# Mixing the heads of an attention score on quarters of the TensorE array, with keys in chunks of 128, 128, 128 and 64

## Chip, cores and metric

One NeuronCore of a Trainium2 chip runs the whole program in one launch. The metric is the device time of that launch in microseconds (us), lower is better; a time is the median of several runs.

## What is computed

Talking-heads attention feeds a mixture of experts (`moe`) and a second one (`moe2`). The change lies wholly in the attention:

```python
batch, n_heads, seq, head_dim = (4, 12, 448, 64)
scores = scale * np.matmul(q, k.transpose(0, 1, 3, 2))
scores = np.einsum('bhij,hg->bgij', scores, w_pre)      # pre-mix over the 12 heads
scores = scores - np.max(scores, axis=-1, keepdims=True)
attn = np.exp(scores)
attn = attn / (np.sum(attn, axis=-1, keepdims=True) + 1e-09)
attn = np.einsum('bhij,hg->bgij', attn, w_post)         # post-mix over the 12 heads
return np.matmul(attn, v).astype(np.float32)
```

All in float32. The result, 1792 tokens of 768 features, goes to `_moe_ref` and `_moe2_ref`, which stay as they are.

## The kernel before

`phase_a` is the attention, and the later phases are the two mixtures. Tokens are taken in tiles of at most 120 (three of 120 and one of 90 for each of the 4 batches, 16 in all). For a tile:

- `q_prep` and `k_prep` turn q (and, once a batch, k) with TensorE transposes and split them in a high and a low part; `scores` (L367) multiplies them in three matmuls for each head, two heads at a time on the two row halves of the array.
- Each head's scores (tokens x 448 keys) are copied to SBUF (`ss`) and sorted by a DMA (L386) into `s2`, so that 120 partitions hold 10 tokens x 12 heads. 12 such units of 10 tokens make a tile (9 in the short one), 180 in all.
- `pre` (L417) mixes the heads of one unit: one 120 x 120 matmul with the block matrix `kron_pre` over 448 keys. `top` (L420, VectorE) takes the maximum of each row, `exp` (L424, ScalarE) the exponential and its sum.
- Three units (30 tokens) make a group. `fin` (L440 to L442, VectorE) divides the block matrix of the post-mix by the sums, which gives `wc`. `post` (L455) has the exponentials of a chunk of 112 keys as weights and `wc` as the moving operand, so that the result has keys on partitions; 4 chunks x 3 units = 12 matmuls of 120 columns for a group, 720 in all. Each chunk of a group is copied from PSUM to `am` (L228 on VectorE, L229 on ScalarE).
- When a tile is whole, `av_mul` (L481) multiplies with v: 12 heads x 4 chunks, two heads side by side on the two column halves of the array.

Beside this, `narrow` turns the float64 weights of the first mixture to float32 in 64 pieces (DMA in, four to six small instructions on ScalarE, VectorE and POOL, DMA out).

A float32 matmul is two records in the trace, each with its weight load; a matmul on a part of the array runs beside its neighbours on the other parts.

The order on every engine is made by `Plan.schedule`: each operation has a cost, a due time (counted in groups), the buffers that it takes and the operations that it depends on; the engine that is free first takes the ready operation that is due first. The costs and due times say only in which order the instructions are written; each engine then runs its own list in order and waits at semaphores. `mode` names how the array is split ("" whole, "rows", "cols"), and `STAY` puts off an operation that would change it. PSUM has 8 banks, dealt out as 2 for `pre`, 2 for `post` and 4 for the rest.

The program begins with `build_kron`, which loads the two small mixing matrices with DMAs issued by ScalarE and builds the block matrices on VectorE.

## Time and profile before

| | us |
|---|---|
| time before, median of 3 runs (893.16 to 899.93) | 894.21 |
| the profiled execution, its own time | 892.66 |
| its span in the trace | 890.9 |
| of it the attention, to the first matmul of the first mixture | 487.4 |
| TensorE (PE) busy in the attention | 471.26 |
| VectorE (DVE) busy in the attention | 366.48 |
| ScalarE (ACT) busy in the attention | 337.42 |

The page of the profile gives busy times by engine and by line for the whole span. The later phases begin at 487.4 us, so the tables by stretch of time tell the stages apart; the timeline shows instructions one after the other with the idle time ahead of each and what ended it; the table of waits sums that idle time by what was waited for. PEld is TensorE's weight load, which runs beside the matmul. The end of a matmul is modelled, so what one costs in a row of its like is read from start to start: a merged row of n records that lasts T, with a mean duration d of one record, has (T - d) / (n - 1) from one start to the next.

### The profile page before, as it was taken

What the parts mean: (1) busy time and instruction counts of PE and PEld (TensorE: products, weight loads), DVE (VectorE), ACT (ScalarE), POOL (GpSimd) and SP (SyncE); (2) the same over time, 40 slices, a digit from 0 to 9 for tenths busy, and PEclk for the clock granted to TensorE, in tenths of its full rate; (3) what the DMA queues carried; (4) which work ended last, traced back from release to release, by engine and by line L of the source; (5) the groups of instructions that cost most, each with busy time, mean ns of one, the idle gap of its engine ahead of it and who ended that gap; (6) DMA issues with size and microseconds to landing.
All of it is one profiled execution on the core that took longest, in us unless ns stands there. A gap on an engine that the chain in (4) does not pass through costs nothing.

```text
span 890.9 us, 17763 instructions
## 1 busy us (share of the span) xinstructions
PE 839.7 (94%) x6636; PEld 606.2 (68%) x6636; DVE 622.2 (70%) x1279; ACT 501.6 (56%) x1119; POOL 180.3 (20%) x275
## 2 busy tenths in 40 slices
PE   7798999999999999999999999999999998989764
PEld 5576777787677777777678767776776787834112
DVE  4658788788977689787844878876777888833003
ACT  5557768666867676776755444454445556502003
POOL 2323344334533344334400000000000000010000
PEclk9999999999999999999999999999999999999878
DMA  7999988998999997999576792553554458899998
GB/s 164 205 195 240 226 239 223 255 233 185 218 236 247 233 235 201 227 228 235 161 210 139 185 192 79 183 189 118 176 186 143 142 183 249 309 349 414 415 375 310
DMA packets 179666, 198.92 MB, mean 223 GB/s; under 512 B 71296, under 2 KB 153186, under 8 KB 179580
## 3 DMA queue, kind: packets, MB, share of 16 engines
q1 hardware_dynamic: 164824, 159.18, 62.0%
q0 software_dynamic: 14496, 38.60, 19.9%
q8 instruction: 52, 0.85, 0.4%
q14 instruction: 34, 0.28, 0.1%
q10 hardware_dynamic: 260, 0.01, 0.0%
HBM read 135.40 MB, written 23.59 MB: 178 GB/s over the span
## 4 chain that ended last, share of the span: by engine, by line
PE 72%; DMA 12%; DVE 6%; ACT 4%; SPq 3%; issue 2%; POOL 1%; ACTq 0%; DVEq 0%; POOLq 0%
PE po L455 13%; PE pre L417 12%; PE h L715 8%; PE av L481 8%; PE h L716 7%; PE h L718 7%; PE s L367 5%; DMA s<-ss 4%; PE eh L1095 2%; DMA wf<-w 2%; DMA raw<-in_moe_w_in_dram 2%; PE p L837 2%; DMA ring<-in_moe_w_dram 2%; DMA early<-in_moe_w_dram 1%; SPq L1002 1%
## 5 line engine op out<-in xcount | busy, mean ns | idle before, releaser
L455 PEld LDWEIGHTS po<-wc,e 120*112 120x112 f32 x1440 | 171.7, 177 | 65.7 <-issue 46.0
L455 PE MATMUL po<-wc,e 120*112 120x120 f32 x1440 | 183.4, 269 | 3.3 <-ACT am L229 2.5
L417 PE MATMUL pre<-s,kron_pre 120*120 120x448 f32 x360 | 167.8, 552 | 6.0 <-ACT e L424 4.2
L420 DVE TENSOR_REDUCE mz<-pre 120x1 f32<-120x448 f32 x180 | 111.4, 620 | 49.8 <-PE pre L417 48.5
L715 PE MATMUL h<-x,wh 128*128 128x512 f32 (+1 forms) x384 | 139.7, 373 | 3.4 <-ACT wh L667 3.4
L716 PE MATMUL h<-x,wh 128*128 128x512 f32 (+1 forms) x384 | 136.7, 365 | 0.0
L424 ACT ACTIVATE e<-pre,mz 120x448 f32<-120x448 f32 x180 | 114.6, 637 | 27.6 <-DVE mz L420 25.8
L386 POOL DMA_DIRECT2D s<-ss x180 | 106.3, 592 | 112.9 <-ACT ss L229 72.8
L229 ACT COPY am<-po 112x360 f32<-112x360 f32 x183 | 84.3, 462 | 50.7 <-PE po L455 49.1
L557 POOL TENSOR_TENSOR nar<-nar,cvt 128x384 uint32<-128x384 uint32 x64 | 64.0, 1000 | 146.1 <-DVE cvt L548 59.8
L715 PEld LDWEIGHTS h<-x,wh 128*128 128x128 f32 x384 | 72.2, 188 | 30.9 <-ACT cg L729 9.2
L718 PE MATMUL h<-x,wf 128*128 128x512 f32 (+1 forms) x384 | 87.8, 364 | 0.0
L729 ACT ACTIVATE cg<-h 128x512 int32<-128x512 f32 (+1 forms) x64 | 34.6, 541 | 92.3 <-PE h L718 92.3
L716 PEld LDWEIGHTS h<-x,wh 128*128 128x128 f32 x384 | 72.2, 188 | 11.2
L481 PE MATMUL av<-am,v 112*64 112x120 f32 (+1 forms) x1536 | 77.6, 261 | 0.0
L481 PEld LDWEIGHTS av<-am,v 112*64 112x64 f32 x1536 | 74.1, 137 | 2.1 <-issue 0.3
L718 PEld LDWEIGHTS h<-x,wf 128*128 128x128 f32 x384 | 66.7, 188 | 11.9
L730 DVE SCALAR_TENSOR_TENSOR cg<-h,cg 128x512 f32<-128x512 f32 (+1 forms) x64 | 39.6, 619 | 46.1 <-ACT cg L729 46.1
L417 PEld LDWEIGHTS pre<-s,kron_pre 120*120 120x120 f32 x360 | 52.5, 183 | 22.1 <-ACT e L424 13.7
L668 DVE TENSOR_TENSOR wf<-wf,wh 128x768 fp32r<-128x768 f32 x64 | 61.0, 953 | 9.2 <-ACT wh L667 9.1
L737 ACT ACTIVATE cg<-cg,consts 128x512 f32<-128x512 f32 (+1 forms) x64 | 42.9, 671 | 35.9 <-DVE cg L732 35.6
L229 ACT COPY ss<-s 120x448 f32<-120x448 f32 (+1 forms) x114 | 55.6, 537 | 10.7 <-DMA s<-ss 8.0
(173 smaller groups left out, 1138.4 us busy)
## 6 DMA issues: line engine op xcount, KB each, us to landing
s<-ss POOLq DMA_DIRECT2D x144, 210.0 KB, 8.4
early<-in_moe_w_dram SPq DMA_DIRECT2D x36, 768.0 KB
wf<-w SPq DMA_DIRECT2D x64, 384.0 KB
raw<-in_moe_w_in_dram SPq DMA_DIRECT2D x32, 384.0 KB
w<-nar SPq DMA_DIRECT2D x64, 192.0 KB
raw<-in_moe_w_out_dram SPq DMA_DIRECT2D x32, 384.0 KB
gn<-in_moe_w_dram SPq DMA_DIRECT2D x16, 768.0 KB
early<-w SPq DMA_DIRECT2D x16, 384.0 KB
```

What stands on the lines that cost most here:

```text
L229: return nc.scalar.copy(out=out, in_=in_)
L386: QUEUE[e].dma_start(out=s2t[ti][h::12, :n // 10], in_=x[h][:n])
L417: nc.tensor.matmul(prt[gi, c][:, :S], kpre, s2t[ti][:, 3 * g + c, :], start=True, stop=True)
L420: nc.vector.tensor_reduce(out=mz[gi][:, 0, c:c + 1], in_=prt[gi, c][:, :S], axis=AX.X, op=ALU.max, negate=True)
L424: nc.scalar.activation(out=et[gi][:, c, :], in_=prt.pop((gi, c))[:, :S], func=AF.Exp, bias=mz[gi][:, 0, c:c + 1], accum_out=mz[gi][:, 1, c ...
L455: nc.tensor.matmul(pt[:, :360].rearrange("p (g i) -> p g i", i=30)[:, :, 10 * c:10 * c + 10], et[gi][:, c, jt * CJ:(jt + 1) * CJ], wct[gi] ...
L481: nc.tensor.matmul(pt[64 * o:64 * o + 64, x * 120:x * 120 + n], vt[:, g, jt, :], am[ti % 2][:, g, jt, :n], start=(jt == 0), stop=(jt == NJ ...
L557: nc.gpsimd.tensor_tensor(out=f, in0=f, in1=x["t"], op=ALU.add)
L668: nc.vector.tensor_tensor(out=wf_t[v], in0=wf_t[v].bitcast(F32), in1=wh.bitcast(F32), op=ALU.subtract)
L715: nc.tensor.matmul(pt, wh[:, c], xh[:, c, :], start=(c == 0), stop=False)
L716: nc.tensor.matmul(pt, wh[:, c], xl[:, c, :], start=False, stop=False)
L718: nc.tensor.matmul(pt, wl[:, c], xh[:, c, :], start=False, stop=(c == 5))
```

## The change

Four things are changed together:

- **Pre-mix on quarters.** The sorted scores stand on partitions 4 to 123, and the 4 partitions before them are filled with zeros once. So the first 5 tokens of a unit end at partition 63 and the other 5 begin at 64. `pre` takes two units at once as four matmuls of 64 columns (60 of them in use), each on one quarter of the array: row half r holds 5 tokens of each unit, column half u is the unit. The results lie in two PSUM banks with 120 rows in use of 128. 88 such pairs and 4 single units (whole array) take the place of 180 matmuls.
- **Keys in chunks of 128, 128, 128 and 64.** `post` runs over three full chunks; the chunk of 64 (`post_half`) is made for two groups at once, six heads on each column half of the array. `av_mul` has three full chunks and, ahead of them, the half chunk on quarters of the array. k and v are loaded and turned in the same chunks.
- **Groups of 40 tokens** (of 20, 30 or 40 in the short tile): 48 groups in place of 60. `fin`, the copies and `wc` are as much wider.
- **PSUM banks by the plan.** All 8 banks are one pool; the planner gives each operation the bank that is free first, at most 6 for `pre`, 3 for `post` and 4 for the rest. Due times are set anew.

Matmuls, by the built programs: `pre` 180 before, 352 on quarters (88 sets of four) and 4 whole after; `post` 720 before, 540 with 128 keys and 360 with 64 keys (180 side by side pairs) after; `av` 768 before, 576 and 192 on quarters (48 sets of four) after; scores and transposes of q as before. Copies to `am`: 240 before (183 on ScalarE, 57 on VectorE), 180 after (137 and 43). In the list of TensorE the way in which the array is split changes 123 times before the first mixture begins, and 207 times after the change.

The core of the diff ("..." where lines are left out):

```diff
-PLACES = {"pre": 2, "post": 2, "ps": 4, "knat": 2, "qnat": 2, "ssrc": 8, "s2": 2, "e": 3, "wc": 2, "xst": 1,
-          "raw": 4, "nar": 5, "cv_t": 3}
-SPARE = 3 * ["ps", "pre", "ps", "post", "ps", "pre", "ps", "post"]
-
-K_DUE, S_DUE, S_SPAN, P_DUE, AV_DUE, AV_SPAN, STAY = 5.6, 4.8, 1.9, 1.9, 0.0, 1.0, 0.6
+PLACES = {"knat": 2, "qnat": 2, "ssrc": 8, "s2": 2, "e": 5, "mz": 4, "wc": 2, "xst": 1, "raw": 4, "nar": 5, "cv_t": 3}
+BANKS, MOST = 8, {"pre": 6, "post": 3, "ps": 4}
+
+K_DUE, S_DUE, S_SPAN, P_DUE, AV_DUE, AV_SPAN, STAY = 4.8, 4.8, 2.5, 2.45, 0.3, 0.5, 0.45
...
-N_FIRST, N_LAST = 5.5, 55.0
+PAIRED = 2
+N_FIRST, N_LAST = 5.5, 56.5
...
-    nc.scalar.dma_start(out=wb, in_=w.unsqueeze(0).to_broadcast([10, 12, 12]))
+def build_kron(nc, pool, ident, w, scale, name, inner):
...
+    wb = pool.tile([128, 12], F32, name=f"wb_{name}")
+    nc.vector.memset(wb, 0.0)
+    m = pool.tile([128, 2, 5], F32, name=f"m_{name}")
+    for u in range(2):
+        p = slice(64 * u, 64 * u + 60) if inner else slice(4 + 60 * u, 64 + 60 * u)
+        nc.scalar.dma_start(out=wb[p], in_=w.unsqueeze(0).to_broadcast([5, 12, 12]))
+        nc.vector.tensor_reduce(out=m[:, u], in_=ident[:, p].rearrange("p (i h) -> p i h", i=5), axis=AX.X, op=ALU.add)
     if scale != 1.0:
         nc.vector.tensor_scalar(out=wb, in0=wb, scalar1=scale, scalar2=None, op0=ALU.mult)
...
+    kr = pool.tile([128, 120 if inner else 128], F32, name=f"kron_{name}")
+    if inner:
+        out = [(kr.rearrange("p (g i) -> p g i", i=10), m.rearrange("p u i -> p (u i)"))]
+    else:
+        nc.vector.memset(kr, 0.0)
+        out = [(kr[:, 64 * u:64 * u + 60].rearrange("p (i g) -> p g i", i=5), m[:, u]) for u in range(2)]
...
 
     ROWS = [120, 120, 120, 90]
-    NG = [4, 4, 4, 3]
+    UNITS = [[[2, 2], [2, 2], [2, 2]]] * 3 + [[[2, 2], [2], [2, 1]]]
...
+        s2 = [sg.tile([128, 12, S], F32, name=f"s2_{i}") for i in range(2)]
+        nc.vector.memset(s2[0][:4], 0.0)
+        nc.gpsimd.memset(s2[1][:4], 0.0)
+        vh = sl.tile([2 * HJ, H // 2, D], F32, name="v_half")
...
+        amt = [sl.tile([CJ, 120 * H * NJ + 60 * H], F32, name=f"am{i}") for i in range(2)]
+        am = [t[:, :120 * H * NJ].rearrange("p (g t i) -> p g t i", g=H, t=NJ) for t in amt]
+        ah = [t[:, 120 * H * NJ:].rearrange("p (g i) -> p g i", g=H // 2) for t in amt]
...
-            return PSUMS[slot.tag_used].tile([128, 512], F32, tag=slot.tag_used, name=name)
+            return ps.tile([128, 512], F32, tag=f"bank{slot.bank}", name=name)
...
+                n, keys = (CJ, slice(t, CJ * NJ, NJ)) if t < NJ else (HJ, slice(CJ * NJ, S))
                 nc.sync.dma_start(
-                    out=knat[b, half][:, t],
-                    in_=k[b, 6 * half:6 * half + 6, t::NJ, :].rearrange("h p d -> p h d"))
-            kload[b, half, t] = dma(0.55, 0.9, start, due=due, late=3.0 if b else 0.0, takes=[] if t else [kslot[b, half]],
+                    out=knat[b, half][:n, t],
+                    in_=k[b, 6 * half:6 * half + 6, keys, :].rearrange("h p d -> p h d"))
...
+                if c < 3:
+                    ins = nc.sync.dma_start(
+                        out=vt[:, 4 * c:4 * c + 4],
+                        in_=v[b, 4 * c:4 * c + 4, :CJ * NJ].rearrange("h (p t) d -> p h t d", t=NJ))
+                else:
+                    x = c - 3
+                    ins = nc.sync.dma_start(
+                        out=vh[HJ * x:HJ * x + HJ],
+                        in_=v[b, 6 * x:6 * x + 6, CJ * NJ:].rearrange("h p d -> p h d"))
...
-                    QUEUE[e].dma_start(out=s2t[ti][h::12, :n // 10], in_=x[h][:n])
+                    QUEUE[e].dma_start(out=s2[ti % 2][4 + h:124:12, :n // 10], in_=x[h][:n])
...
+            ti, c0, us = groups[gi]
+            c, n = c0 + sum(us[:x]), us[x]
+            b = [Slot("pre") for _ in range(n)]
+            el[gi, x] = Slot("e")
+            if x == 0:
...
-                nc.tensor.matmul(prt[gi, c][:, :S], kpre, s2t[ti][:, 3 * g + c, :], start=True, stop=True)
...
-            m = plan.op([("PE", 0.76)], mul,
-                        [sorted_[ti, h] for h in range(H)], due, behind=[mixed[gi]] if c else [],
-                        takes=[b] + ([el[gi]] if c == 0 else []), uses=[s2l[ti]] + ([] if c == 0 else [el[gi]]))
...
+                prt[gi, x] = [bank(s, f"pre{gi}_{x}_{r}") for r, s in enumerate(b)]
+                if n == 1:
+                    nc.tensor.matmul(prt[gi, x][0][:, :S], kpre[:124], s2[ti % 2][:124, c, :], start=True, stop=True)
+                    return
+                for u in range(2):
+                    for r in range(2):
+                        p = slice(64 * r, 64 + 60 * r)
+                        nc.tensor.matmul(prt[gi, x][r][64 * u:64 * u + 64, :S], kpre[p, 64 * r:64 * r + 64],
+                                         s2[ti % 2][p, c + u, :],
+                                         start=True, stop=True)
...
+            m = plan.op([("PE", 0.76)], mul, [sorted_[ti, h] for h in range(H)], due,
+                        behind=[mixed[gi]] if x else [], takes=b + [el[gi, x]] + ([] if x else [mzl[gi]]),
+                        uses=[s2l[ti]] + ([mzl[gi]] if x else []), mode="quads" if n == 2 else "")
...
+            for r in range(n):
+                t = plan.op([("DVE", 0.54)], top(r), [m], due, uses=[b[r], mzl[gi]])
+                expd[gi, x, r] = plan.op([("ACT", 0.63)], exp(r), [t], due, uses=[b[r], el[gi, x], mzl[gi]])
...
-                wct[gi] = sl.tile([120, 3, 120], F32, tag="wc", name=f"wc{gi}", bufs=PLACES["wc"])
-                z, rz = mz[gi][:, 1], mz[gi][:, 2]
+                wct[gi] = sl.tile([128, 4, 120], F32, tag="wc", name=f"wc{gi}", bufs=PLACES["wc"])
...
-                pt = made["po", gi, jt] = bank(b, f"po{gi}_{jt}")[:CJ]
-                for c in range(3):
-                    nc.tensor.matmul(
-                        pt[:, :360].rearrange("p (g i) -> p g i", i=30)[:, :, 10 * c:10 * c + 10],
-                        et[gi][:, c, jt * CJ:(jt + 1) * CJ], wct[gi][:, c, :], start=True, stop=True)
+                pt = made["po", gi, jt] = bank(b, f"po{gi}_{jt}")
+                for ex, w, where in shares(gi):
+                    nc.tensor.matmul(place(pt[:, :120 * n], H, n, where), ex[:, jt * CJ:(jt + 1) * CJ], w,
+                                     start=True, stop=True)
 
...
+            m = plan.op([("PE", 0.21 * n)], mul, [f], due, takes=[b], uses=held(gi))
+            amdone[gi, jt] = plan.op([("ACT", 0.12 + 0.08 * n), ("DVE", 0.1 + 0.12 * n)], out, [m] + am_free(ti), due,
...
+        def post_half(gis, fs, due):
+
...
+                    for ex, w, where in shares(gi):
+                        for o in range(2):
+                            r = slice(HJ * o, HJ * o + HJ)
+                            nc.tensor.matmul(place(pt[r, cols], H // 2, ns[x], where), ex[:, CJ * NJ:],
+                                             w[:, 60 * o:60 * o + 60], start=True, stop=True)
...
+            m = plan.op([("PE", 0.05 + 0.11 * sum(ns))], mul, fs, due, takes=[b],
+                        uses=[z for gi in gis for z in held(gi)], mode="cols")
...
+                for x in range(3):
+                    for o in range(2):
+                        for r in range(2):
+                            rows = slice(HJ * r, HJ * r + HJ)
+                            nc.tensor.matmul(pts[r][64 * o:64 * o + 64, x * 120:x * 120 + n], vh[rows, 2 * x + o, :],
+                                             ah[ti % 2][rows, 2 * x + o, :n], start=(x == 0), stop=False)
...
-                        g = 2 * (XS * s + x) + o
-                        nc.tensor.matmul(pt[64 * o:64 * o + 64, x * 120:x * 120 + n], vt[:, g, jt, :],
-                                         am[ti % 2][:, g, jt, :n], start=(jt == 0), stop=(jt == NJ - 1))
+                        g = 6 * s + 2 * x + o
+                        nc.tensor.matmul(made["av", ti][s][64 * o:64 * o + 64, x * 120:x * 120 + n], vt[:, g, jt, :],
+                                         am[ti % 2][:, g, jt, :n], start=False, stop=(x == 2 and jt == NJ - 1))
...
+                    for x in range(len(us)):
+                        pre(gi, x, at[gi] - P_DUE + sum(us[:x]) / 3)
+                    f = fs[gi] = fin(gi, at[gi] - (0.7 if odd else 0.4))
                     for jt in range(NJ):
-                        post(gi, jt, f, gi + jt / 4)
+                        post(gi, jt, f, at[gi] + (jt + odd) * sum(us) / 12)
+                    if odd:
+                        post_half([gi - 1, gi], [fs[gi - 1], f], at[gi] - 0.25)
+                    elif gi == last:
+                        post_half([gi], [f], at[gi] + 0.75 * sum(us) / 3)
```

On TensorE, in the middle of the attention before, `pre` (L417, one unit) alternates with `post` (L455, one chunk), all of them on the whole array:

```order
L417 MATMUL pre_2_5562<-s_14_4994,kron_pre 120x448
L455 MATMUL po_0_5566<-wc_5482,e_5393 112x12x10 x3
L417 MATMUL pre_0_5573<-s_14_4994,kron_pre 120x448
L455 MATMUL po_1_5577<-wc_5482,e_5393 112x12x10 x3
L417 MATMUL pre_1_5582<-s_14_4994,kron_pre 120x448
L455 MATMUL po_2_5590<-wc_5482,e_5393 112x12x10 x3
L455 MATMUL po_3_5595<-wc_5482,e_5393 112x12x10 x3
L417 MATMUL pre_2_5601<-s_14_4994,kron_pre 120x448
L455 MATMUL po_0_5604<-wc_5584,e_5474 112x12x10 x3
```

At such a place after the change, four matmuls on quarters (L468, 64 rows of output) stand between the chunks of `post` (L545, 128 rows), and the half chunk of two groups (L570, column halves) follows:

```order
L545 MATMUL po_1_4455<-wc_4389,e_1_4321 128x12x2x5 x2
L545 MATMUL po_2_4467<-wc_4389,e_0_4130 128x12x2x5 x2
L545 MATMUL po_2_4467<-wc_4389,e_1_4321 128x12x2x5 x2
L468 MATMUL pre_0_0_4481<-s_1_110,kron_pre 64x448
L468 MATMUL pre_0_1_4482<-s_1_110,kron_pre 64x448
L468 MATMUL pre_0_0_4481<-s_1_110,kron_pre 64x448
L468 MATMUL pre_0_1_4482<-s_1_110,kron_pre 64x448
L570 MATMUL ph_4494<-wc_4389,e_0_4130 64x6x2x5 x4
L570 MATMUL ph_4494<-wc_4389,e_1_4321 64x6x2x5 x4
L376 MATMUL qt_0_4507<-ident,qnat_4314 128x120 x2
L545 MATMUL po_0_4510<-wc_4472,e_0_4399 128x12x2x5 x2
L545 MATMUL po_0_4510<-wc_4472,e_1_4415 128x12x2x5 x2
```

What was one kind of matmul after the other now goes from the whole array to quarters, to column halves and back within a few microseconds.

On VectorE, the program before begins with the two block matrices and then the low part of the first q (L345):

```order
L44 TENSOR_SCALAR wb_pre<-wb_pre 120x12
L46 TENSOR_REDUCE m_pre<-ident 120x10
L49 TENSOR_TENSOR kron_pre<-wb_pre,m_pre 120x12x10
L46 TENSOR_REDUCE m_post<-ident 120x10
L49 TENSOR_TENSOR kron_post<-wb_post,m_post 120x120
L345 TENSOR_TENSOR q_lo<-qt_0_125,q_hi 128x2x9x10
L309 TENSOR_TENSOR k_lo<-kt_0_133,k_hi 128x448
```

After the change the same stretch has four more small fills and the zeros of `s2` (L230, 4 partitions of 5376) ahead of the first q (L385):

```order
L44 MEMSET wb_pre 128x12
L49 TENSOR_REDUCE m_pre<-ident 128x5 x2
L51 TENSOR_SCALAR wb_pre<-wb_pre 128x12
L56 MEMSET kron_pre 128x128
L60 TENSOR_TENSOR kron_pre<-wb_pre,m_pre 128x12x5 x2
L44 MEMSET wb_post 128x12
L49 TENSOR_REDUCE m_post<-ident 128x5 x2
L60 TENSOR_TENSOR kron_post<-wb_post,m_post 128x120
L230 MEMSET s_0_109 4x5376
L385 TENSOR_TENSOR q_lo<-qt_0_132,q_hi 128x2x9x10
L349 TENSOR_TENSOR k_lo<-kt_0_140,k_hi 128x448
```

ScalarE likewise issues four small loads of the mixing matrices ahead of its first copy of q, in place of two.

## Rows read from the trace of the kernel before

**Rows 1.** Stretches: us, busy PE, PEld, DVE, ACT, POOL (x instructions), clock, DMA share, GB/s.

```profile
0.00:100.00 100.00, 85.63 (x678) 61.88 (x678) 63.64 (x138) 60.59 (x147) 32.95 (x56) 1.00 1.02 207
100.00:450.00 350.00, 348.37 (x3060) 266.61 (x3056) 285.56 (x634) 254.21 (x651) 141.15 (x201) 1.00 0.92 222
0.00:487.40 487.40, 471.26 (x4130) 359.49 (x4130) 366.48 (x811) 337.42 (x852) 174.98 (x258) 1.00 0.93 216
```

**Rows 2.** The same for the stretch in which DVE is busiest.

```profile
200.00:250.00 50.00, 49.12 (x423) 37.10 (x423) 46.41 (x101) 36.05 (x92) 21.84 (x31) 1.00 0.88 205
```

**Rows 3.** PE's waits from 100 us to 487 us: us, times, longest.

```profile
PE pre L417 <- ACT e L424: 0.6, 1, 0.6
PE po L455 <- ACT am L229: 0.6, 1, 0.6
PE kt L300 <- DVE k_lo L309: 0.2, 1, 0.2
```

**Rows 4.** Timeline of PE, end of the attention: start, us, instruction, records.

```profile
477.55 5.90 PE L455 MATMUL po<-wc,e 120*112 120x120 f32 x48
483.38 4.10 PE L481 MATMUL av<-am,v 112*64 112x90 f32 x96
487.40 0.50 PE L715 MATMUL h<-x,wh 128*128 128x512 f32 x1
```

**Rows 5.** Timeline of PE, scores to post-mix to av.

```profile
150.36 0.36 PE L367 MATMUL s<-k_lo,q_hi 64*120 64x448 f32 x2
150.56 0.37 PE L367 MATMUL s<-k_hi,q_lo 64*120 64x448 f32 x2
150.86 0.87 PE L455 MATMUL po<-wc,e 120*112 120x120 f32 x6
...
152.32 0.78 PE L455 MATMUL po<-wc,e 120*112 120x120 f32 x6
152.93 0.92 PE L417 MATMUL pre<-s,kron_pre 120*120 120x448 f32 x2
153.69 0.78 PE L455 MATMUL po<-wc,e 120*112 120x120 f32 x6
154.39 5.14 PE L481 MATMUL av<-am,v 112*64 112x120 f32 x96
```

**Rows 6.** Groups by line and shape in the attention: busy us, mean ns, idle before.

```profile
L455 PE MATMUL po<-wc,e 120*112 120x120 f32 x1440 | 183.4, 269 | 3.3 <-ACT am L229 2.5 <-DVE wc L442 0.5
L417 PE MATMUL pre<-s,kron_pre 120*120 120x448 f32 x360 | 167.8, 552 | 6.0 <-ACT e L424 4.2 <-ACT ss L229 1.7
L481 PE MATMUL av<-am,v 112*64 112x120 f32 x1152 | 61.7, 267 | 0.0
L481 PE MATMUL av<-am,v 112*64 112x90 f32 x384 | 15.9, 242 | 0.0
L228 DVE COPY am<-po 112x360 f32<-112x360 f32 x57 | 29.8, 528 | 9.3 <-PE po L455 9.2
```

**Rows 7.** Timeline of PE: matmuls on sixteenths of the array (32 rows, 32 columns).

```profile
597.75 1.85 PE L837 MATMUL p<-gn 32*32 32x512 f32 x44
```

**Rows 8.** Timeline of PE: 128-column weights under 32 moving columns.

```profile
501.48 0.97 PE L704 MATMUL wtr<-st,gn 128*128 128x32 f32 x8
```

**Rows 9.** Timeline of ACT at the start; ACTq is a DMA being issued.

```profile
0.75 1.38 ACTq L42 DMA_DIRECT2D wb_pre<-in_w_pre_dram  x1
2.16 0.78 ACTq L42 DMA_DIRECT2D wb_post<-in_w_post_dram  x1
2.98 1.28 ACT L229 ACT_TABLE_LOAD   x1 [2.98 <-issue]
```

**Rows 10.** Timeline of DVE at the start.

```profile
5.58 0.28 DVE L49 TENSOR_TENSOR kron_post<-wb_post,m_post 120x120 f32<-120x120 f32 x1 [1.19 <-DMA wb_post<-in_w_post_dram]
5.79 0.47 DVE L345 TENSOR_TENSOR q_lo<-qt,q_hi 128x180 fp32r<-128x180 f32 x1
8.23 2.12 DVE L309 TENSOR_TENSOR k_lo<-kt,k_hi 128x448 fp32r<-128x448 f32 x3 [1.98 <-ACT k_hi L229]
```

296 lines of the change are left out of this document (173 added, 123 removed).

## Prediction, made before the changed kernel ran

> **What bounds the kernel now.** I read the table by stretches of time first. In the attention TensorE is busy 471.26 us of 487.40, and between 100 and 450 us it is busy 348.37 of 350.00, while VectorE is busy 285.56 and ScalarE 254.21 [rows 1]. The table of waits then says who holds TensorE up after the first 100 us: three waits of 0.6, 0.6 and 0.2 us [rows 3]. So the attention is bound by TensorE's own list, and its length is the sum of what stands in that list, plus some 14.4 us of idleness in the first 100 us (100.00 less 85.63) [rows 1]. The mixtures follow without a pause: their first matmul starts at 487.40, as the last av ends its row [rows 4]. Nothing in them is changed, so I forecast the change of the attention alone and add it to the profiled execution's own time, 892.66 us, which is 1.6 us under the median of the runs, 894.21.
>
> The timeline gives the prices, from start to start. A `pre` is 0.76 us (152.93 to 153.69); three matmuls of `post` are 0.61 us (152.32 to 152.93), so one is about 0.204 us and one of its two records 0.102 [rows 5]. One record of `av` is (5.14 - 0.27) / 95 = 0.051 us with 120 columns [rows 5, 6] and (4.10 - 0.24) / 95 = 0.041 with 90 [rows 4, 6]; as two stand side by side, a pair of records is 0.103 or 0.081.
>
> **The change part by part.**
>
> *Pre-mix.* 180 x 0.76 = 136.8 us now. Afterwards there are 88 sets of four quarter matmuls and 4 whole ones. If all four of a set run together, a set streams the same 448 columns as one `pre` did, 0.76, and I add 0.01 for the staggered starts: 88 x 0.77 + 4 x 0.76 = 70.8. That is -66.0 us. No row shows quarters. The nearest is finer: on sixteenths of the array 44 records of 512 columns take 1.85 us [rows 7], where one record alone would take 512 / 448 x 0.38 = 0.43 us and 44 in a row 19. So at least ten were under way at once, with several on the same rows and several on the same columns. I take four abreast. The other end, two abreast, is a rival below.
>
> *Post-mix.* 1440 records [rows 6] x 0.102 = 146.9 us now. After: 540 matmuls of 128 keys, 1080 records with weights of 128 columns in place of 112. The moving operand stays at 120 columns, so 0.102 is the lower end. The upper end comes from a row with 128-column weights and only 32 moving columns: eight records in 0.97 us, so between (0.97 - 0.28) / 7 = 0.099 and, if the first two weights were there already, / 6 = 0.115 [rows 8]; there the weight load sets the pace. I take 0.11: 118.8 us (110.2 to 124.2). The 180 pairs of half chunks are 360 pairs of records with 60 moving columns. Lower end: half of a record of 120 columns, 0.051. Upper end: the pair of `av`, 0.103, within which two 64-column weight loads are known to fit. I take 0.058, half of the upper figure for 128-column weights, since the two loads go to different column halves: 20.9 us (18.4 to 37.1). Together 139.7, so -7.2 us.
> The Trainium skill (TensorEngine Tiling (Array Packing), Instruction Overhead) says that each matmul carries about 60 cycles of overhead, and warns against splitting a dimension that is small already. By it, as an estimate at 2.4 GHz, the 360 short pairs would cost 25 ns more each, 9 us in all. The `av` row does not bear that out for 120 columns, since 0.103 us leaves no such gap; for 60 columns no row here shows it, and the sum goes without.
>
> *av.* 1152 x 0.051 + 384 x 0.041 = 74.5 us now. Three chunks of four remain, 55.9; the half chunk is 48 sets of four (36 with 120 columns, 12 with 90) of two records: 36 x 0.206 + 12 x 0.162 = 9.4. That is -9.2 us.
>
> So the streamed part of TensorE's list falls by 66.0 + 7.2 + 9.2 = 82.4 us.
>
> *Changes of the array's split.* There are 123 now and 207 after, 84 more. One is priced by a place where scores end: the next `post` starts 0.30 us after the last pair of scores (150.56 to 150.86) instead of the usual 0.20, and its six records take 0.87 us instead of 0.78 [rows 5], so 0.19. The lower end is the first part alone: `av` starts at 154.39, where six records of 0.102 from 153.69 would have let it start at 154.30, 0.09 late [rows 5]. The upper end is all of TensorE's busy time that I can't place: 471.3 less the three kinds above (358.2), less, by TensorE's list, 288 pairs of scores at 0.20 (57.6) and 218 transposes at no more than 0.11 (24), is 31.5 us, 0.26 for each of 123. I take 0.19: +16.0 us (+7.6 to +21.8).
>
> *The start.* ScalarE issues four small loads in place of two; the second took 0.78 us [rows 9], so what follows is some 1.6 us later, and VectorE's `kron_post`, which waits for the last of them, with it. Then VectorE fills 4 x 5376 zeros ahead of the first `q_lo`. No row shows a fill. Three subtractions of 448 columns took 2.12 us [rows 10], 1.6 ns a column, which would make 8.5 us; as a fill reads nothing I allow a quarter of that, 2.1, as the lower end. Queued behind it stand the first `q_lo` (5.79) and the first `k_lo` (8.23) [rows 10], for which the first scores on TensorE wait, and so everything. They come at about 5.9 + 1.6 + (2.1 to 8.5) + 0.5 = 10.1 to 16.5 instead of 8.2: 1.9 to 8.3 us late. I take +4. POOL's own fill has no such neighbour: nothing sorted needs POOL until the scores are there.
>
> *The first 100 us.* There TensorE waits 14.4 us for loads, exponentials and sorted scores, and a shorter matmul partly makes the wait longer. The first fifth of the attention would hold some 14 us of the net 66 saved; I let 4 go (0 to 8).
>
> *Hidden.* VectorE loses 14 of its 57 copies (29.8 us [rows 6]), each wider, so at most 7 us; and 12 `fin` fall away. ScalarE loses 46 copies. Both were not waited for [rows 3] and are priced at nothing, as long as TensorE's list covers them (rival 1). Four more loads a batch (two of k, two of v) lie on SP's queue, beside TensorE's list. Sets of four need two PSUM banks free at once; `pre` may now hold six, so this too is priced at nothing.
>
> **Sum.** -82.4 + 16.0 + 4 + 4 = -58.4, so 892.66 - 58.4 = 834.3. I predict 834 us, with an attention of about 429 us.
>
> **Rivals.**
>
> 1. *VectorE and ScalarE become the pace.* In 100 to 450 us VectorE is busy 285.56 us [rows 1] and would still be so for about 279. My forecast shrinks this stretch to about 300 us, a share of 0.93, against 0.82 now. For it: TensorE's waits would come back as waits of `pre` for the exponentials and of `post` for `wc`. Against: between 200 and 250 us VectorE stands at 46.41 of 50, 0.93, and TensorE is busy 49.12 all the same [rows 2]. If no more than 0.87 can be held, the stretch is 321 us, 21 longer, and the time 855. The Trainium skill (TensorEngine Tiling (Array Packing), PSUM Bottleneck) states this as a rule: tiling speeds up TensorE and not the emptying of PSUM, which may become the bottleneck.
> 2. *The quarters run two abreast, not four.* Then a set costs 1.52 us, the 88 sets and 4 singles 136.8, and the pre-mix saves nothing: -58.4 + 66.0 = +7.6, 900 us, slower than before. It decides from a set of 0.77 + 58.4 / 88 = 1.43 us on. The sixteenths speak against it [rows 7]; what remains for it is that a quarter reads 64 rows and not 32.
> 3. *The DMA engines become the bound.* Their share is 0.93 over the attention [rows 1]; the same transfers in 429 us would be 1.06. If it can't pass 1.0, the attention is 453 us and the time 858. Against: the first 100 us have a share of 1.02 [rows 1], and a packet's time grows when another queue's packets stand beside it, so the share is no measure of a limit.
>
> **How the numbers follow.** My forecast has 0.78 and its own range, 814 to 850: all lower ends at once give 892.66 - 82.4 - 8.6 - 2.5 + 7.6 + 1.9 = 809, the upper ones 892.66 - 82.4 + 5.4 + 16.2 + 21.8 + 8.3 + 8 = 870, and neither set is likely to fall together. Rival 1 has 0.11, rival 2 0.06, rival 3 0.03, and 0.02 is left for what I have not seen. The range for 8 in 10 is 814 to 858, which takes in the nearer part of rivals 1 and 3. A measurement of this kernel can tell about 1% from no change. Faster by over 1% (under 885): the forecast and rivals 1 and 3, 0.92. Rival 2 lies at +0.8% and is split: within 1% 0.05, slower 0.03.
>
> **What would show it.** A set of `pre` on quarters with all four records starting within some 0.03 us and the next set or matmul 0.77 us on: the first term. Records of `post` 0.11 us apart, pairs of the half chunk 0.058: the second. 0.19 us lost at each change of split. `q_lo` near 12 us. TensorE busy over 95% from 100 us on and no long waits for ACT or DVE: rival 1 is out. The forecast is wrong if `pre` and `post` wait for `mz`, `e` or `wc` in many places, or if a set takes 1.5 us.

## The result, and the profile after

The changed kernel takes 888.28 us (median of 12 runs, 882.26 to 895.33), the kernel before, run beside it, 896.61 (12 runs): ratio 0.990 [0.988, 0.993], one per cent faster where 6.6% was forecast. The profiled execution of after took 882.26 us (span 880.1), 10.4 less than the profiled one of before. It is the fastest of the 12 runs of after. Its attention lasts 472.3 us in place of 487.4, which is 15.1 less and not 58.4; the mixtures that follow take 4.3 us more (407.8 for 403.5).

The table by stretches of the changed kernel (us, busy PE, PEld, DVE, ACT, POOL, clock, DMA share, GB/s):

```profile
0.00:100.00 100.00, 75.52 (x660) 52.35 (x661) 60.87 (x125) 52.36 (x128) 31.24 (x49) 0.95 0.90 182
100.00:450.00 350.00, 331.67 (x3886) 250.04 (x3887) 289.05 (x621) 255.69 (x646) 146.47 (x207) 0.99 0.94 229
0.00:472.30 472.30, 425.34 (x4842) 318.19 (x4842) 363.64 (x773) 322.75 (x805) 180.58 (x259) 0.98 0.92 218
```

Beside [rows 1] TensorE's busy time is 45.9 us shorter (471.26 to 425.34), but it now stands idle 47.0 us where it stood 16.1. Between 100 and 450 us, where it had 1.6 us of idleness, it has 18.3. Over the whole attention VectorE and ScalarE are no busier. And TensorE's granted clock, 1.00 all through the attention before, is 0.98: in five stretches, some 20 us together, it is at 1.2 GHz and not 2.4, which costs up to 10 us. Each of them follows waits. One of the five, after 10 us with 2.2 us of idleness:

```profile
203.00:213.00 10.00, 7.82 (x59) 3.30 (x56) 9.76 (x20) 6.70 (x20) 5.74 (x9) 0.99 0.91 262
213.00:216.00 3.00, 3.00 (x15) 1.00 (x12) 2.43 (x7) 2.35 (x9) 1.35 (x2) 0.50 0.64 191
```

Where [rows 3] had three waits, there are now these, of PE and of its weight load, from 100 to 472 us (us, times, longest):

```profile
PEld s L407 <- ACT e L484: 14.3, 21, 2.6
PEld po L545 <- ACT e L484: 13.0, 12, 2.4
...
PE po L545 <- DVE wc L506: 7.4, 6, 1.9
PE s L407 <- ACT e L484: 4.7, 11, 1.9
```

`post` waits for its moving operand `wc` and for exponentials; scores wait until an exponential has been taken, which I read as a wait for the PSUM bank that it is taken from. A wait of the weight load is not by itself idle time of TensorE: before the change the weight loads of `pre` waited 7.0 us in 22 places for exponentials beside a TensorE that was busy 348.37 of 350 us.

The prices of single matmuls were close all the same. PE's timeline after the change, to be held against [rows 5]:

```profile
120.10 0.68 PE L570 MATMUL ph<-wc,e 128*64 128x60 f32 x16
120.72 3.24 PE L468 MATMUL pre<-s,kron_pre 64*64 64x448 f32 x32
123.88 0.46 PE L407 MATMUL s<-k_hi,q_hi 64*120 64x448 f32 x2
...
127.22 2.92 PE L545 MATMUL po<-wc,e 128*128 128x120 f32 x24
129.98 0.37 PE L376 MATMUL qt<-ident,qnat 120*128 120x120 f32 x2
130.28 1.15 PE L570 MATMUL ph<-wc,e 128*64 128x60 f32 x32
131.36 0.84 PE L605 MATMUL av<-am,v_half 64*64 64x120 f32 x24
132.13 3.91 PE L611 MATMUL av<-am,v 128*64 128x120 f32 x72
135.97 0.98 PE L468 MATMUL pre<-s,kron_pre 64*64 64x448 f32 x8
```

32 records of `pre` are four sets (each of the four matmuls has two records); from 120.72 to the next instruction at 123.88 they take 3.16 us, 0.79 for a set with the change of split at the end. 24 records of `post` go in 2.76 us (127.22 to 129.98), 0.115 for one with a change of split in it. Of `ph`, 32 records last 1.15 with 0.23 for one, so a pair comes every 2 x (1.15 - 0.23) / 31 = 0.059 us. 72 records of `av` take 3.84 (132.13 to 135.97), a pair 0.107.

### The profile page after: what moved, and what is told of

Read it like the earlier page. It is cut to its first block, busy times and chain, and to the rows that moved or that the text cites. A ratio compares the mean times of both kernels' runs of the same rounds, so it can differ in the third digit from the quotient of the medians.

```text
span 880.1 us, 19108 instructions
## 1 busy us (share of the span) xinstructions
PE 797.0 (91%) x7348; PEld 565.9 (64%) x7348; DVE 616.5 (70%) x1239; ACT 485.4 (55%) x1070; POOL 185.9 (21%) x276
## 5 line engine op out<-in xcount | busy, mean ns | idle before, releaser
L545 PE MATMUL po<-wc,e 128*128 128x120 f32 x1080 | 140.9, 283 | 11.3 <-DVE wc L506 9.0
L545 PEld LDWEIGHTS po<-wc,e 128*128 128x128 f32 x1080 | 129.1, 195 | 34.2 <-ACT e L484 16.2
L484 ACT ACTIVATE e<-pre,mz 128x448 f32<-128x448 f32 x180 | 112.4, 639 | 34.8 <-DVE mz L476 34.4
L476 DVE TENSOR_REDUCE mz<-pre 128x1 f32<-128x448 f32 x180 | 101.0, 615 | 21.1 <-PE pre L468 20.9
L687 POOL TENSOR_TENSOR nar<-nar,cvt 128x384 uint32<-128x384 uint32 x64 | 64.5, 1008 | 139.2 <-DVE cvt L678 53.1
L468 PE MATMUL pre<-s,kron_pre 64*64 64x448 f32 (+1 forms) x704 | 86.3, 575 | 4.8 <-DMA s<-ss 3.2
L261 ACT COPY am<-po 128x480 f32<-128x480 f32 (+2 forms) x110 | 58.5, 538 | 24.0 <-PE po L545 23.1
L261 ACT COPY ss<-s 120x448 f32<-120x448 f32 (+1 forms) x117 | 60.7, 539 | 13.0 <-DMA s<-ss 6.6
L611 PE MATMUL av<-am,v 128*64 128x120 f32 (+1 forms) x1152 | 59.6, 262 | 0.5 <-issue 0.5
L810 ACT CAST wh<-wf 128x768 fp32r<-128x768 f32 x64 | 52.9, 826 | 10.9 <-DMA wf<-w 10.9
```

The costliest lines, as they stand in the source:

```text
L261: return nc.scalar.copy(out=out, in_=in_)
L468: nc.tensor.matmul(prt[gi, x][r][64 * u:64 * u + 64, :S], kpre[p, 64 * r:64 * r + 64], s2[ti % 2][p, c + u, :], start=True, stop=True)
L476: nc.vector.tensor_reduce(out=mz[gi][:, 0, i:i + 1], in_=prt[gi, x][r][:, :S], axis=AX.X, op=ALU.max, negate=True)
L484: nc.scalar.activation(out=et[gi, x][:, r, :], in_=prt[gi, x][r][:, :S], func=AF.Exp, bias=mz[gi][:, 0, i:i + 1], accum_out=mz[gi][:, 1, i ...
L545: nc.tensor.matmul(place(pt[:, :120 * n], H, n, where), ex[:, jt * CJ:(jt + 1) * CJ], w, start=True, stop=True)
L611: nc.tensor.matmul(made["av", ti][s][64 * o:64 * o + 64, x * 120:x * 120 + n], vt[:, g, jt, :], am[ti % 2][:, g, jt, :n], start=False, sto ...
```

## The experiments

Attention lengths come from one profiled execution each; two executions of one order (the runs e7 and e11 below) lay 3.6 us apart, so differences under about 4 us are not read. That is the least that must be allowed for: the 12 runs of after spread over 13 us, and no trace tells how much of it lies in the attention. "Idle" is the attention less TensorE's busy time in it. The DMA share adds up the times of all packets and can pass 1. The order "given" is that of the changed kernel, "fast" that of e1; "few bytes" is the edit of e2. In the runs with few bytes and in e3, e5b and e9 the mixtures read other data, so only their attention is compared.

| run | order of the lists | left out or changed | attention | idle | DMA share | kernel, this execution |
|---|---|---|---|---|---|---|
| before | before | | 487.4 | 16.1 | 0.93 | 892.66 |
| after | given | | 472.3 | 47.0 | 0.92 | 882.26 |
| e2 | given | few bytes | 478.5 | 46.4 | 0.64 | 890.56 |
| e1 | fast | | 479.5 | 53.1 | 0.94 | 893.66 |
| e5 | fast | few bytes | 446.5 | 31.8 | 0.70 | 858.02 |
| e12 | fast, start and end mended | few bytes | 440.7 | 25.4 | 0.71 | 853.90 |
| e3 | given | no conversion | 457.6 | 33.7 | 0.99 | 861.06 |
| e9 | given | conversion on a constant | 473.7 | 43.6 | 0.95 | 877.80 |
| e5b | fast | no conversion | 477.8 | 46.0 | 0.95 | 881.85 |
| e4 | given | whole `pre` | 500.3 | 25.4 | 0.87 | 914.20 |
| e10 | fast | few bytes, whole `pre` | 493.3 | 23.8 | 0.61 | 906.95 |
| e15 | before | few bytes | 483.1 | 11.4 | 0.63 | 889.57 |

### Order and transfers: e1_fast_wire, e2_few_bytes, e5_wire_and_bytes

Three theories stood against each other: TensorE waits because the planner, which counts 424 us of transfers and itself ends the attention at 447.7, wrote their time into the order (pace); because the DMA engines are full (transfers); because VectorE and ScalarE empty PSUM too slowly (emptying).

e1, in `Plan.schedule` (`wire` is the time at which the planner takes its transfers to be done):

```diff
-                wire = max(wire, end) + o.moves
+                wire = max(wire, end) + 0.8 * o.moves
```

The planner also chooses the engine of some operations, so VectorE has 805 instructions in the attention of e1 and ScalarE 770, where after has 773 and 805; the array's split changes 229 times and not 207.

e2, in `narrow` (e5 has both edits; `blank` are four buffers that POOL fills with ones at the start, in 2.79 us):

```diff
-                x["raw"] = sn.tile([128, UP, 2], U32, tag="raw", name=f"raw{u}", bufs=PLACES["raw"])
-                nc.sync.dma_start(out=x["raw"].rearrange("p n k -> p (n k)"),
-                                  in_=src.bitcast(U32)[:, 2 * c0:2 * (c0 + UP)])
+                x["raw"] = blank[u % PLACES["raw"]]
+                nc.sync.dma_start(out=x["raw"].rearrange("p n k -> p (n k)")[:, :16],
+                                  in_=src.bitcast(U32)[:, 2 * c0:2 * c0 + 16])
...
-                nc.sync.dma_start(out=dst[:, c0:c0 + UP], in_=x["f"])
+                nc.sync.dma_start(out=dst[:, c0:c0 + 8], in_=x["f"][:, :8])
```

> Only a number of the planner is changed: it takes every transfer as lasting 0.8 of what it is given. No instruction is added or left out, only the order moves. The planner's own end of the attention falls from 447.7 to 396.2 us, since in the changed kernel's plan the transfers fill 424 of 438 us and TensorE stands idle 77 us. Theory 'pace' (the order is written for transfers that are slower than the chip's; the idle is written into the order): the attention lasted 472.3 us, 24.6 more than its plan; with the same excess it comes to about 421, and the kernel to about 832 (820 to 845). Theory 'transfers' (the DMA engines bound the attention): they carry the same bytes, so the attention stays at 460 to 475 and the kernel at 875 to 890, with more waits of pre for sorted scores. Theory 'emptying' (VectorE and ScalarE bound it through the PSUM banks): their lists are as long as before, 440 to 460 us of attention, 850 to 870.

> Left out: 46 of 48 columns of each transfer in and out by which the weights of the first mixture become float32 (64 pieces), so those transfers remain as instructions in the same order but with 1/48 of the bytes; the mixtures read other data of the same size. About 38 of the attention's 100 MB are gone. Theory 'transfers': the DMA share of 0.92 falls to about 0.6 and the attention from 472 to 430 or less. Theory 'pace': the order is the same and its idle with it, 465 to 475. Theory 'emptying': as VectorE and ScalarE do the same, 465 to 475.

> The order of the kernel with the planner's transfers at 0.8, and with 46 of 48 columns of the weight transfers left out (the mixtures read other data). Each of the two alone left the attention where it was (479.5 and 478.5 us against 472.3). Theory 'order and transfers in turn' (the order leaves idle for the transfers' time; an order without that idle then waits for q, which comes late because the DMA engines are full): the 26 us of waits for q of the fast order go, and with them most of its half clock, so attention 425 to 445 us. Theory 'emptying' (VectorE, at 47 of 50 us in that order, is the bound): 455 or more, with waits for wc, exponentials and PSUM banks.

Measured: e1 892.93 us, ratio to before 0.994 [0.990, 0.999], attention 479.5; e2 attention 478.5; e5 attention 446.5 (858.02 us in its one run). All three lie just outside the ranges of the theory that they come nearest to, e1 and e2 some 4 us above 475, e5 1.5 above 445. No theory alone is right: for e1 "transfers" comes nearest, for e2 "pace" and "emptying", whose range was the same. With the order as given, 37 MB less of transfers gain nothing: e2 has the same waits of `post` for `wc` (7.8 us) and of scores for exponentials (4.9) as after. With the order made for faster transfers these nearly go, and others take their place. PE's waits of e1 after 100 us:

```profile
PE qt L376 <- DMA qnat<-in_q_dram: 15.2, 2, 8.7
PE po L545 <- DVE wc L506: 2.5, 4, 1.2
```

The longer of the two, on PE's timeline of e1:

```profile
297.91 2.04 PE L545 MATMUL po<-wc,e 128*128 128x120 f32 x16
308.70 0.53 PE L376 MATMUL qt<-ident,qnat 90*128 90x90 f32 x2 [8.74 <-DMA qnat<-in_q_dram]
```

SP's timeline of e1 ahead of it (SPq is a DMA being issued):

```profile
291.96 4.90 SPq L690 DMA_DIRECT2D w<-nar  x1
296.91 5.39 SPq L306 DMA_DIRECT2D qnat<-in_q_dram  x6
302.41 0.35 SPq L659 DMA_DIRECT2D raw<-in_moe_w_out_dram  x1
```

And the stretches of e1 around both waits, after one that runs well:

```profile
100.00:150.00 50.00, 49.77 (x602) 38.29 (x601) 46.98 (x97) 36.77 (x91) 21.94 (x32) 1.00 0.89 220
180.00:200.00 20.00, 13.53 (x158) 10.78 (x158) 12.49 (x27) 9.43 (x25) 7.68 (x11) 0.83 1.14 223
295.00:315.00 20.00, 11.26 (x112) 9.04 (x113) 10.63 (x23) 6.07 (x16) 6.49 (x10) 0.74 1.05 187
```

The loads of q for the next tile are issued in 5.39 us, behind a store whose issue took 4.90, while the DMA engines stand at a share of 1.05. TensorE waits 8.74 us, and the granted clock of the stretch is 0.74. In the first stretch the share is 0.89, and the same kind of order keeps TensorE busy 49.77 of 50 us beside a VectorE at 46.98. With few bytes (e5) the waits for q after 100 us are gone:

```profile
100.00:446.50 346.50, 337.67 (x4166) 259.25 (x4165) 318.80 (x673) 254.31 (x640) 147.44 (x208) 1.00 0.66 145
```

From e1 to e5 the attention falls by 33.0 us: 21.3 less idle, and 11.7 less busy at a clock of 0.99 in place of 0.96. So the given order, and the fast order with its full transfers, each hold the attention at some 475 us. "Emptying" is out as the cause in the fast order: VectorE is busy 0.92 of the stretch and TensorE 0.97.

### The conversion of the weights: e3_no_convert, e9_convert_apart, e5b_wire_no_convert

In e3 the operations `size` to `plus` of `narrow` emit nothing, `raw` has 8 buffers, and the store is changed; e5b is e3 in the order of e1. In e9 they run on a constant, the loads have 7 buffers of their own, and the store sends what was loaded, as in e3; to make room, `cv_t` has 2 buffers in place of 3 and `nar` 3 in place of 5. The store of e3:

```diff
-                nc.sync.dma_start(out=dst[:, c0:c0 + UP], in_=x["f"])
+                nc.sync.dma_start(out=dst.bitcast(U32)[:, c0:c0 + UP], in_=x["raw"].rearrange("p n k -> p (n k)")[:, :UP])
```

> Left out: the small instructions on VectorE, ScalarE and POOL that turn those weights to float32; the transfers stay (what goes out is the raw first half of what came in), and the order of all other instructions is the same. VectorE loses some 80 us and ScalarE some 40 of work in the attention. Theory 'emptying': TensorE's waits for PSUM banks and exponentials (47 us in all) shrink by half or more, attention 435 to 450. Theory 'pace': the waits shrink only by what the small instructions delayed the maxima, 5 to 12 us, attention 460 to 467. Theory 'transfers': 470 or more.

> Why was the attention 14.7 us shorter without the conversion (457.6) in the given order? Here the conversion's instructions run in full, but on a constant; the transfers run in full, but from buffers of their own (7 in place of 4), and what goes out is what came in (the mixtures read other data). So VectorE, ScalarE and POOL have their work again, and no load waits until a conversion has left its buffer. If the work was the cause: 468 to 478 us of attention. If it was that loads on SP's queue wait for VectorE and POOL, and hold the later ones: 454 to 463.

> The same order with the bytes kept and the conversion's small instructions left out (what is stored is the raw first half; the mixtures read other data). VectorE has some 80 us less to do. Theory 'order and transfers in turn': the waits for q stay (15 us or more after the first 100 us), attention 450 to 470. Theory 'emptying': they were late only because VectorE and ScalarE were, attention 420 to 440.

Measured: 457.6, 473.7 and 477.8 us of attention. The first lies between the ranges of "emptying" and "pace", the second in that of the work, the third above both of its ranges. In the given order the conversion's instructions cost 15 us. That it is their work and not the loads that wait for them is what e9 speaks for: no load waits for the conversion there, and it is as slow as after, with the same waits of `post` for `wc` (7.6 us, 6 times). What its fewer buffers cost was not measured apart. In e3 TensorE's waits for `wc` and for exponentials nearly go (1.2 and 0.5 us after 100 us), and loads are what it waits for most, beside a DMA share of 1.01. The largest of its waits after 100 us, and the stretch:

```profile
PE qt L376 <- DMA qnat<-in_q_dram: 5.3, 3, 2.6
```

```profile
100.00:457.60 357.60, 345.93 (x4179) 266.19 (x4177) 209.24 (x432) 233.94 (x591) 87.26 (x149) 0.99 1.01 245
```

In the fast order leaving them out gains nothing (479.5 to 477.8), although VectorE then has 102 us less to do: the DMA share is 0.95, with waits for k and sorted scores (3.8 and 2.3 us after 100 us). I had expected 15 us or more of waits for q there; they are 0.3. The same transfers, without the conversion, take 457.6 us of attention in the given order and 477.8 in the fast one, so they set no fixed length either. Whether VectorE's or ScalarE's part of the conversion is what delays the given order was not tried.

### The quarters undone: e4_whole_pre, e10_whole_few_bytes

```diff
                 for u in range(2):
-                    for r in range(2):
-                        p = slice(64 * r, 64 + 60 * r)
-                        nc.tensor.matmul(prt[gi, x][r][64 * u:64 * u + 64, :S], kpre[p, 64 * r:64 * r + 64],
-                                         s2[ti % 2][p, c + u, :],
-                                         start=True, stop=True)
+                    nc.tensor.matmul(prt[gi, x][u][:, :S], kpre[:124], s2[ti % 2][:124, c + u, :], start=True, stop=True)
...
-                    yield et[gi, x][:, r, :], wct[gi][:, i, :], (10 * sum(us[:x]) + 5 * r, 2 * n - 1)
+                    yield et[gi, x][:, r, :], wct[gi][:, i, :], (10 * i, 1)
```

> The quarters alone are undone: a pair of units is two whole matmuls with the 124 x 128 block matrix instead of four on quarters; order, chunks, groups and banks stay. TensorE's own list grows by 88 x 0.76 = 67 us, less about 100 changes of the split at 0.19 = 19, net 48. If TensorE were still the pace (my forecast), the attention grows by all 48, to 520. If the order leaves idle that the longer matmuls fill (47 us of waits, 12 of half clock, 17 of small waits), it grows by 10 to 30, to 482 to 502.

> The quarters undone (two whole matmuls for a pair of units) in the fast order with few bytes in the weight transfers (the mixtures read other data), where the attention took 446.5. TensorE's list grows by 88 x 0.76 = 67 us, less some 30 changes of the split at 0.19 = 6. In the given order undoing them cost 28. If, without the transfers, TensorE is the pace, as my forecast had it: 495 to 508. If VectorE, ScalarE or the planner's order are: 450 to 475.

In the given order the quarters are worth 28.0 us (500.3 against 472.3; e4 took 914.20 us in its one run). I had put the list's growth at 48; it has only 31 changes of split fewer, so it is 67 - 31 x 0.19 = 61. Of these 61 us, 33 do not show: 21.6 lie in time that TensorE would have stood idle (47.0 to 25.4 us), and its busy time grows by 49.6 and not by 61, in part because the clock is 0.99 and not 0.98. In the fast order with few bytes they are worth 46.8 (493.3 against 446.5), and there TensorE is the pace again. The stretch of e10:

```profile
100.00:493.30 393.30, 391.44 (x3925) 297.72 (x3925) 330.33 (x684) 264.04 (x652) 150.37 (x213) 1.00 0.57 131
```

1.9 us of idleness in 393. So there my picture of TensorE's list held, without the weight transfers and in an order made for that. The 493.3 lie just under the 495 to 508 that I had expected, the 500.3 of e4 within 482 to 502.

### Control and floor: e15_before_few_bytes, e12_ends_wire_bytes

e15 is the kernel before with e2's edit; e12 is e5 with the start and end as e6 has them (next section).

> The kernel before the change with 46 of 48 columns of the weight transfers left out (the mixtures read other data). There TensorE was busy 348.4 of 350 us. If the transfers became a limit only with the change: 484 to 488 us of attention, as before. If they held the kernel before as well: 475 or less.

> The fast order and few bytes again, with the mended start and end. If nothing but the transfers and the start stood between the changed kernel and the attention of 429 us that I forecast, this comes to 434 to 442 (446.5 less 6 to 8 for the start and 3 for the end, which the fast order no longer had). If there is another bound near 446: 444 to 448.

Before the change 37 MB less gain 4.3 us (483.1, just under the 484 to 488 that I had expected of a TensorE that is the pace), in waits of the first 100 us, and TensorE is busy as before from there on (e15):

```profile
100.00:450.00 350.00, 349.65 (x3086) 268.35 (x3085) 285.46 (x634) 254.44 (x652) 141.42 (x201) 1.00 0.55 129
```

So the transfers, at a share of 0.93 with all their bytes, held up nothing after the first 100 us. With few bytes, the fast order and the mended start and end the changed kernel comes to 440.7 us, 12 from my 429.

### The start and the end: e6_start_end, e13_fills_first

VectorE's timeline at the start of the changed kernel, where [rows 10] stood before:

```profile
6.51 0.07 DVE L44 MEMSET wb_post<- 128x12 f32 x1
6.58 0.20 DVE L49 TENSOR_REDUCE m_post<-ident 128x5 f32<-128x60 f32 x1
11.67 0.28 DVE L60 TENSOR_TENSOR kron_post<-wb_post,m_post 128x120 f32<-128x120 f32 x1 [4.89 <-DMA wb_post<-in_w_post_dram]
13.02 4.54 DVE L230 MEMSET s<- 4x5376 f32 x1 [1.06 <-issue]
17.48 0.40 DVE L385 TENSOR_TENSOR q_lo<-qt,q_hi 128x180 fp32r<-128x180 f32 x1
```

ScalarE's, for [rows 9]:

```profile
6.61 1.50 ACTq L48 DMA_DIRECT2D wb_post<-in_w_post_dram  x2
```

And PE's waits from 468 to 490 us, at the first matmuls of the mixture, which use the banks of the last `av`:

```profile
PE h L858 <- ACT xst L261: 3.2, 1, 3.2
PE h L858 <- DVE xst L260: 2.0, 1, 2.0
```

In e6 `load_kron` is the memset and the two loads of `build_kron`; `take(x, 4)` gives a bank out of the upper four:

```diff
-        kpre = build_kron(nc, sg, ident, w_pre, 0.125, "pre", False)
+        wbs = load_kron(nc, sg, w_pre, "pre", False), load_kron(nc, sg, w_post, "post", True)
...
-        nc.vector.memset(s2[0][:4], 0.0)
+        nc.gpsimd.memset(s2[0][:4], 0.0)
...
-            plan.take(x)
+            plan.take(x, 4)
```

e13 is e7 (below) with both memsets of `s2` ahead of `build_kron`, the first on VectorE again.

> Two places of the changed kernel are mended and the plan stays: at the start the small matrices' four loads are issued at once and the zeros of the first s2 are written by POOL, not by VectorE ahead of the first q_lo; at the end the last av takes banks out of the upper four, so that the first matmul of the mixture need not wait for the copies of av. The first pass of scores with k_lo stood at 18.4 us, 8.6 later than before the change; it should stand near 10. If that delay runs through, the attention is 8 us shorter; if the waits for loads at 34 and 66 us swallow it, 0 to 4. The end gives 3 to 5 (waits of 3.4 and 2.0). Attention 459 to 469, kernel 868 to 880.

> The kernel with mended start and end and the planner's transfers at 0.95, but the zeros of the first s2 are written by VectorE at the very start, while it waits for the small matrices (idle from 1.7 to 5.9 us), and POOL writes only those of the second. With both fills on POOL, VectorE's small multiplication of the pre-mix matrix took 4.49 us instead of 0.17 and ended as POOL's fills must have; the first k_lo came at 11.62. If POOL's fill holds that instruction: it takes 0.2 us again, the first pass of scores with k_lo starts at 8.5 to 9.5 instead of 12.3, attention 458 to 461 in place of 461.9 to 465.5, kernel 872 to 877. If VectorE was held by something else: 12.3 stays.

e6 takes 881.28 us, 0.981 [0.976, 0.987], attention 469.7. The first k_lo pass of scores starts at 12.3 in place of 18.4, and the two waits of h are gone, but little of the 6 us runs through: a wait for q that ended at 71.0 us and took 5.0 now ends at 68.3 and takes 6.2. Both the attention and the time lie just above what I had expected (459 to 469, 868 to 880). e13 brings the pass from 12.3 (in e7) to 10.7 and the first `pre` from 32.9 to 29.2, and again a later wait takes it: the attention is 461.6, where e7 has 461.9. The 10.7 lies between what I had expected for a VectorE that is free (8.5 to 9.5) and one that is held (12.3). The largest of PE's waits of e13 in the first 100 us:

```profile
PE qt L383 <- DMA qnat<-in_q_dram: 11.8, 3, 7.6
```

SP's timeline of e13 ahead of the longest, at 58 us:

```profile
40.58 6.17 SPq L295 DMA_DIRECT2D knat<-in_k_dram  x2
46.80 10.92 SPq L313 DMA_DIRECT2D qnat<-in_q_dram  x2
57.76 6.01 SPq L295 DMA_DIRECT2D knat<-in_k_dram  x2
```

Two loads of q need 10.92 us to be issued; the DMA share from 40 to 66 us is 1.12. What TensorE reaches earlier waits for the same transfers. e13 has the lowest time of the kernels that compute the whole result, 875.00 us, 0.974 [0.969, 0.979] of before; e7 and e11 are within its noise.

The end's gain moves too. In e13 the wait of the first h for the copies of `av` is replaced by one for weights that ScalarE has not copied (PE, 461 to 512 us):

```profile
PE h L865 <- ACT wh L817: 6.2, 2, 4.5
PE pw L844 <- DVE early L838: 0.7, 1, 0.7
```

ScalarE's copy waits in turn for their load:

```profile
480.59 0.84 ACT L817 CAST wh<-wf 128x768 fp32r<-128x768 f32 x1 [3.43 <-DMA wf<-w]
```

The mixtures take 409.4 us there, 403.5 before.

### Planner's figures and buffers: e7_ends_wire95, e11_more_raw, e14_true_costs

e7 is e6 with

```diff
-                wire = max(wire, end) + o.moves
+                wire = max(wire, end) + 0.95 * o.moves
...
-                        load_q(ti, p // 2, d - K_DUE - 2 if ti == 0 else d - 2.1, mark)
+                        load_q(ti, p // 2, d - K_DUE - 2 if ti == 0 else d - 3.1, mark)
```

e11 is e7 with 6 buffers for `raw`; e14 is e13 with `TURN` 0.19 in place of 0.095 and `("PE", 0.223 * n)` for `post`.

> As the run before, and the planner takes transfers as 0.95 of what it was given and loads q one group earlier (3.1 instead of 2.1 groups ahead). Its own end falls from 447.7 to about 431. Theory 'order and transfers in turn': the transfers fill 436 us of the DMA engines' time in the attention, so it can come to 445 to 460 and the kernel to 855 to 868; if the waits for q come back as in the fast order, 462 to 475 and 870 to 885.

> The kernel with mended start and end and the planner's transfers at 0.95, as it stands, but with 6 buffers in place of 4 for the raw weights, of which the planner knows nothing: the order is the same. A load of raw weights then need not wait until the conversion has left its buffer, and holds nothing behind it on SP's queue. If that coupling costs time: attention 452 to 459 in place of 461.9, kernel 866 to 873. If not: 460 to 464, kernel 874 to 879.

> As the run before, and the planner counts a change of the array's split as 0.19 us (0.095 before) and a matmul of post as 0.223 (0.21), which the traces show. Theory 'transfers': these are full at 446 of 462 us, so better costs for TensorE can do little, attention 455 to 461, kernel 868 to 877. Theory 'order': the waits of post for wc and of scores for exponentials (15 us) go, attention 444 to 452, kernel 858 to 868.

e7: 877.09 us, 0.980 [0.972, 0.988], attention 461.9 at a DMA share of 0.97. The time is in the range that I had set for a return of the waits for q (870 to 885), but after 100 us none of them is there; TensorE waits for exponentials and `wc`. e11: 877.70, 0.976 [0.969, 0.982], attention 465.5, so more buffers give nothing. e14: 880.19, 0.980 [0.974, 0.986], attention 469.8: with TensorE's true costs in the plan the order is no better, and TensorE waits 21.2 us for loads of q and k (11.8 and 9.4). Both theories of e14 had expected a shorter attention (455 to 461, 444 to 452), so both missed; the waits for loads speak for the transfers, and no run shows more than that.

## Why the prediction was wrong

- **What bounds the kernel before**: right. e15 shows TensorE's list as the pace after 100 us, with 0.55 of DMA share or 0.92.
- **Pre-mix, -66.0; post-mix, -7.2; av, -9.2; changes of split, +16.0**: close in their prices (the timeline above). With few bytes and the fast order, undoing the quarters costs 46.8: the 66.9 of the list, less 52 x 0.19 = 9.9 for fewer changes of split, less 8.0 of idleness that it fills, would be 49.0. Together the terms make 404.9 us of busy time for TensorE (471.3 - 82.4 + 16.0), and 4.2 more for the 22 further changes of the fast order. The traces have 425.3 (after) and 414.7 (e5). The half clock explains up to 10 of the 20.4 that are over in after; the rest no row explains. On the half pairs the estimate from the Trainium skill (TensorEngine Tiling (Array Packing), Instruction Overhead) would have had 0.058 + 0.025 = 0.083 us; the trace has 0.059 and does not bear it out here.
- **The start, +4 (1.9 to 8.3)**: mis-sized. The first k_lo pass came 8.6 us late (9.83 to 18.40). The first `q_lo` stands at 17.48 and not near 12. The fill took 4.54, inside my bounds, but I let the loads run on ahead. The second pair is issued only when VectorE has cleared its target, at 6.61, behind a wait for the first.
- **The first 100 us, +4**: idle 24.5 us for 14.4, so +10, the start included, where the two terms had 8.
- **Hidden**: this step failed. I priced the loads, the work of VectorE and ScalarE and the PSUM banks at nothing, as long as TensorE's list covers them. The cover was TensorE's slowness. Between 100 and 450 us it now stands idle 18.3 us where it stood 1.6. In the given order the conversion's work costs 15 us of attention, 13.3 of them idleness (e3); in an order that assumes shorter transfers TensorE waits for q, until the bytes are taken out (e1, e5: 33.0 us). The order itself stands in no term of mine: the plan by which the lists are written ends the attention at 447.7, 19 us above my 429. As to the banks, the first matmuls of the mixture wait 5.2 us for the copies of the last `av`, and scores wait 4.7 for exponentials; that a common pool causes the latter is argued and was not tried. So the sign of being wrong that I had named came in part: `post` waits for `wc` in six places.
- **Rival 3, the DMA engines, 0.03**: the nearest to what the fast order shows, and its 858 us would have been the better forecast, though still 24 under the profiled execution. It is not what holds the kernel as it stands: in the given order few bytes gain nothing (e2). I dismissed it with the claim that a packet's time grows beside other packets, so that the share were no limit. It grows, but by little. The sorted scores' queue (packets' time as a share of 16 engines), in after and in e2:

```profile
q0 software_dynamic: 14384, 38.33, 36.2%
```

```profile
q0 software_dynamic: 14384, 38.33, 33.7%
```

  The same 38.33 MB take 0.362 x 472.3 = 171 us beside the weights and 0.337 x 478.5 = 161 without them, 6% less. So the share was close to a measure: the fullest attention of the study (e3) has 0.99, and the 1.06 of 429 us was reached by no attention here; that it can't be was not shown. That the attention stood at 472, and not at the 453 of this rival, hangs mostly on the conversion's work in the given order: without it, it is 457.6 (e3).
- **Rival 1, VectorE and ScalarE**: half right in one place. In the given order the conversion's instructions cost 15 us (e3, e9). But VectorE reached 0.92 of the 346.5 us after 100 in e5, so 0.87 is no cap, and the 0.83 of after is no bound by itself.
- **Rival 2, two abreast**: out; a set takes 0.79 us and not 1.52.

So of the 43 us that are missing from the attention, 22.9 are idleness above the 24.1 that the forecast left (16.1 + 8), and 20.4 are busy time above 404.9, up to 10 of them half clock after waits. With few bytes, the fast order and the mended start and end 32 of the 43 come back (472.3 to 440.7). How the 32 divide can't be told, since order and transfers each hide the other. Groups of 40 and the common pool of banks were not tried alone.

## What to carry to other kernels

An engine that is busy all the time can cover every other one that is nearly full; before its list is cut by 15%, scale the other shares by the shorter time, and give one that comes out over 1 a large chance until a row refutes it. Where a program writes the order of the lists, ask also what end its own plan has. Where two limits lie close together, removing one can show nothing: test them in pairs. Time won ahead of a full queue can be lost again at its next load, as in e6 and e13, so follow it to the end of the stage before it is counted.
